# A linear attention with two MLPs: weight conversion two chunks at a time, its low parts on VectorE, and gate and attention first in the order

## The chip, the cores and the metric

The kernel runs on one core of one Trainium2 chip. Its time is device microseconds of one execution, median of three runs. The engines are PE (TensorE, with PEld for its weight loads), DVE (VectorE), ACT (ScalarE), POOL (GpSimd) and SP, whose queue issues the DMAs. Engines work through their own instruction lists in order and wait for each other by semaphores.

## The reference

```
q_s = exp(q - max(q, axis=-1));  q_s /= sum(q_s, -1) + 1e-9
k_s = exp(k - max(k, axis=2));   k_s /= sum(k_s, 2) + 1e-9
x   = q_s @ (k_s^T @ v)              # 4 batches, 8 heads, 576 rows, 64 wide
x   = x as (2304, 512)
h   = x @ moe_w_in;   x = (h - tanh(h)) @ moe_w_out       # 512 -> 2048 -> 512
h   = x @ moe2_w_in;  out = softplus(h) @ moe2_w_out
```

All inputs are float64 and the result is float32. The four weight matrices reach the chip as the raw bits of float64 (two 32-bit words a number).

## The kernel before

Every matmul that matters is done as three: an operand is split into a high and a low part (hi, lo, of a rounded 32-bit type), and lo\*hi, hi\*lo and hi\*hi are added up in PSUM.

**Weights.** A matrix comes in 16 chunks of 128 of the 2048 hidden features. A chunk of float64 words is 128 x 1024 words of 32 bits, 512 KB, and lies in one of six buffers of the tag `raw`. `convert` (lines 111 to 126) turns it into 128 x 512 float32 numbers in place by five passes: ACT (L121) reads the top 16 bits, DVE (L122) joins sign and exponent, DVE (L123) clamps, ACT (L124) scales, DVE (L125) shifts the low word in. `parts` (lines 128 to 133) adds a copy on ACT, which is the hi part (L131), and a subtraction, which is the lo part (L132). The lo part runs on POOL, but for every fourth chunk of the first input matrix, where it runs on DVE. `w_task` does a chunk of both matrices of the first MLP, `w2_out_task` a chunk of the last matrix, `w2_in_task` a pair of chunks of the second MLP's input matrix, from which it makes seven sums (a Strassen form) that go back to DRAM.

**Blocks.** The 2304 rows are worked through in five blocks of 512, 256, 512, 512 and 512 columns for the first MLP. A block has 16 steps, one a hidden chunk f: `hidden` (12 matmuls into PSUM tile h), `gate` (ACT tanh L332, DVE g L333, ACT hi part gh L334, DVE lo part gl L335), `mid_out` (12 matmuls into four accumulators x). The hidden product runs two steps ahead of `mid_out`. The first block needs each chunk of the first MLP's weights as it comes to it, so the conversions of the first MLP run beside block 0. The second MLP's input weights are converted beside the blocks that follow, and its output weights beside the last block, in which a converted chunk of the first MLP's output matrix gives up its place.

**Attention.** `kv_task` makes k^T v of a batch and a pair of heads: max over k (DVE L229, then a transposition pm on PE L232, DVE mx L234, a transposition pb L237), subtraction (DVE L239), exp (ACT L240), product pk (PE L244), its reciprocal r (DVE L246, L247), and kv (ACT L250). `x_task` makes a block's x from q: maximum and subtraction (L279, L281), exp (L282), sum (L285 to L287), qn (L289), transposition pt (PE L298), product px (L305), hi and lo part (ACT L307, DVE L308). Those of the first block run ahead of it (the prologue); those of the next block run beside the present one.

**Order.** Tasks are generators that go on by one `yield` a step. A scheduler then lays out each engine's list from the program's order, dependencies and buffers: what comes earlier in the program has the higher priority, and what has its inputs later in its reckoning moves behind. `tc.high_priority()` puts what it encloses ahead.

Of the kernel before, what the change touches and what calls it, by code (L numbers as in the profile page):

```python
# [19 lines left out]
def linear_attention_two_mlps(  # L20
# [28 lines left out]
    nc = tc.nc  # L49
# [39 lines left out]
    def f32(ap):  # L89
        return ap.bitcast(F32)  # L90
# [9 lines left out]
    def raw_tile(name):  # L100
        return main.tile([P, NC, 2 * P], U32, tag="raw", name=name, bufs=6)
# [6 lines left out]
    def load_out(raw, w_out, f):  # L108
        nc.sync.dma_start(out=raw.rearrange("p c f -> p (c f)"), in_=w_out[f * P : (f + 1) * P, :])

    def convert(raw):

        words = raw.rearrange("p c (f two) -> p c f two", two=2)
        y, x = words[:, :, :, 0], words[:, :, :, 1]
        top = raw.bitcast(U16).rearrange("p c (f four) -> p c f four", four=4)[:, :, :, 1]  # L120
# [17 lines left out]
    def w_task(f):
        raws = [raw_tile(f"raw{w}0_{f}") for w in "io"]
        load_in(raws[0], w1_in, f)  # L140
        load_out(raws[1], w1_out, f)
# [60 lines left out]
    def kv_task(b, hp, pool, bufs):  # L202
# [31 lines left out]
        nc.vector.tensor_reduce(mx, pm[:, :KP], axis=AX, op=ALU.max)  # L234
# [10 lines left out]
        r = pool.tile([P, 1], F32, tag="r", name=f"r{nm}", bufs=bufs)  # L245
        nc.vector.tensor_scalar(r, pk[:, P : P + 1], 1e-9, None, op0=ALU.add)  # L246
        nc.vector.reciprocal(r, r)  # L247
        for h in range(2):
            d = slice(h * D, (h + 1) * D)
            nc.scalar.mul(kv[b % 2, hp][d, d], pk[d, d], r[d])  # L250

# [7 lines left out]
    def x_task(i, hp, pool, bufs):  # L259
# [6 lines left out]
        while r0 < n:  # L266
# [28 lines left out]
        yield
# [228 lines left out]
    for f in range(NF):  # L524
        if f >= PRE:
# [166 lines left out]
```

## Time and profile before

| what | us |
|---|---|
| median of three runs | 892.52 (892.36 to 894.33) |
| the profiled execution, its own time | 893.67 |
| its span, first to last instruction | 891.9 |
| PE busy | 841.6 (94%) |
| DVE busy | 637.8 (72%) |
| ACT busy | 489.3 (55%) |
| POOL busy | 93.0 (10%) |

Shares over the whole span hide the stages. Beside block 0 (34 to 158 us) DVE is busy nearly all the time and PE is not; from 300 us to the end of the fourth block PE is busy all the time and DVE under half. A mean duration of a group mixes passes that ran alone with passes that ran beside POOL, so the rows below take one stretch with POOL at work and one without.

### The profile page before, as it was taken

What the parts mean: (1) busy time and instruction counts of PE and PEld (TensorE: products, weight loads), DVE (VectorE), ACT (ScalarE), POOL (GpSimd) and SP (SyncE); (2) the same over time, 40 slices, a digit from 0 to 9 for tenths busy, and PEclk for the clock granted to TensorE, in tenths of its full rate; (3) what the DMA queues carried; (4) which work ended last, traced back from release to release, by engine and by line L of the source; (5) the groups of instructions that cost most, each with busy time, mean ns of one, the idle gap of its engine ahead of it and who ended that gap; (6) DMA issues with size and microseconds to landing.
All of it is one profiled execution on the core that took longest, in us unless ns stands there. A gap on an engine that the chain in (4) does not pass through costs nothing.

```text
span 891.9 us, 11576 instructions
## 1 busy us (share of the span) xinstructions
PE 841.6 (94%) x4152; PEld 721.9 (81%) x4152; DVE 637.8 (72%) x990; ACT 489.3 (55%) x806; POOL 93.0 (10%) x88
## 2 busy tenths in 40 slices
PE   4788889999999999999998999999999999999997
PEld 3566768998888888888886888988899989898986
DVE  8899999899897444434697475667957669675664
ACT  4877776555665332223563565647556466655643
POOL 4243431000000000001242300000100000000000
PEclk9899999999999999999999999999999999999999
DMA  9565655876664210003427254343653444543421
GB/s 248 160 183 170 182 144 145 261 207 186 245 227 134 51 47 12 12 1 118 155 71 249 83 175 112 114 129 113 198 174 111 125 113 124 183 124 111 115 59 71
DMA packets 98616, 121.34 MB, mean 136 GB/s; under 512 B 38656, under 2 KB 62976, under 8 KB 98560
## 3 DMA queue, kind: packets, MB, share of 16 engines
q1 hardware_dynamic: 98560, 120.61, 44.9%
q8 instruction: 33, 0.54, 0.3%
q14 instruction: 23, 0.19, 0.1%
HBM read 96.47 MB, written 24.12 MB: 135 GB/s over the span
## 4 chain that ended last, share of the span: by engine, by line
PE 63%; DVE 15%; issue 8%; DMA 5%; ACT 5%; POOL 3%; SPq 0%; POOLq 0%; ACTq 0%; DVEq 0%
PE h L323 11%; PE one L418 10%; PE o L495 7%; PE o L496 7%; PE o L494 7%; PE seven L418 5%; PE x L352 4%; PE x L350 4%; PE x L351 4%; PE two L418 2%; POOL ol L132 2%; DVE m L229 2%; DVE g L333 1%; DMA rawi<-in_moe_w_in_dram 1%; DVE rawi L122 1%
## 5 line engine op out<-in xcount | busy, mean ns | idle before, releaser
L323 PE MATMUL h<-xh,il 128*128 128x512 f32 (+1 forms) x320 | 126.9, 397 | 9.7 <-DVE g L333 4.4
L323 PE MATMUL h<-xl,ih 128*128 128x512 f32 (+1 forms) x320 | 120.7, 377 | 0.8 <-DVE xl L308 0.8
L323 PE MATMUL h<-xh,ih 128*128 128x512 f32 (+1 forms) x320 | 120.6, 377 | 0.0
L350 PE MATMUL x<-gh,ol 128*128 128x512 f32 (+1 forms) x320 | 119.2, 372 | 0.9 <-DVE x2s L359 0.9
L352 PE MATMUL x<-gh,oh 128*128 128x512 f32 (+1 forms) x320 | 118.7, 371 | 0.0
L351 PE MATMUL x<-gl,oh 128*128 128x512 f32 (+1 forms) x320 | 118.7, 371 | 0.0
L418 PE MATMUL one<-xf,wf 128*128 128x384 f32 x576 | 116.8, 337 | 0.9 <-ACT u L433 0.9
L494 PE MATMUL o<-oh,gl 128*128 128x512 f32 x288 | 112.8, 392 | 2.3 <-DVE gl L479 1.8
L495 PE MATMUL o<-ol,gh 128*128 128x512 f32 x288 | 113.7, 395 | 0.0
L496 PE MATMUL o<-oh,gh 128*128 128x512 f32 x288 | 113.7, 395 | 0.0
L418 PEld LDWEIGHTS one<-xf,wf 128*128 128x128 f32 x576 | 103.0, 188 | 7.4 <-ACT u L433 1.4
L333 DVE TENSOR_TENSOR g<-h,g 128x512 f32<-128x512 f32 (+1 forms) x80 | 50.6, 632 | 53.1 <-ACT g L332 52.9
L332 ACT ACTIVATE g<-h 128x512 f32<-128x512 f32 (+1 forms) x80 | 44.0, 549 | 76.9 <-PE h L323 76.7
L470 DVE TENSOR_SCALAR u<-e 128x768 f32<-128x768 f32 x48 | 26.7, 557 | 80.0 <-ACT e L468 80.0
L323 PEld LDWEIGHTS h<-xh,il 128*128 128x128 f32 x320 | 62.0, 194 | 23.7 <-DVE g L333 5.9
L323 PEld LDWEIGHTS h<-xl,ih 128*128 128x128 f32 x320 | 62.0, 194 | 11.8 <-DVE xl L308 1.6
L478 ACT CAST gh<-e 128x768 fp32r<-128x768 f32 x48 | 40.2, 837 | 56.8 <-DVE e L475 56.2
L323 PEld LDWEIGHTS h<-xh,ih 128*128 128x128 f32 x320 | 61.6, 192 | 10.9
L350 PEld LDWEIGHTS x<-gh,ol 128*128 128x128 f32 x320 | 61.0, 191 | 11.5 <-DVE x2s L359 1.5
L352 PEld LDWEIGHTS x<-gh,oh 128*128 128x128 f32 x320 | 60.9, 190 | 10.2
L351 PEld LDWEIGHTS x<-gl,oh 128*128 128x128 f32 x320 | 60.8, 190 | 10.0
L335 DVE TENSOR_TENSOR gl<-g,gh 128x512 fp32r<-128x512 f32 (+1 forms) x80 | 53.3, 666 | 20.1 <-ACT gh L334 18.9
(97 smaller groups left out, 1534.5 us busy)
## 6 DMA issues: line engine op xcount, KB each, us to landing
wf<-forms SPq DMA_DIRECT2D x168, 256.0 KB, 2.7
rawi<-in_moe_w_in_dram SPq DMA_DIRECT2D x32, 512.0 KB, 4.3
rawo<-in_moe_w_out_dram SPq DMA_DIRECT2D x32, 512.0 KB, 3.4
forms<-stage SPq DMA_DIRECT2D x24, 512.0 KB, 3.2
v<-in_v_dram SPq DMA_DIRECT2D x32, 144.0 KB, 3.9
out_dram<-ot SPq DMA_DIRECT2D x18, 256.0 KB, 3.0
x2d<-x2s SPq DMA_DIRECT2D x16, 256.0 KB, 2.2
k<-in_k_dram SPq DMA_DIRECT2D x24, 144.0 KB, 3.5
```

Of the source, the lines that this page charges most:

```text
L323: nc.tensor.matmul(p, w[:, c], x[:, c, :n], start=at == 0, stop=at == 3 * NC - 1)
L332: tanh[0] = nc.scalar.activation(g, h, AF.Tanh)
L333: nc.vector.tensor_tensor(g, h, g, op=ALU.subtract)
L335: nc.vector.tensor_tensor(gl, g, f32(gh), op=ALU.subtract)
L350: nc.tensor.matmul(a, ol[:, s], gh, start=first, stop=False)
L351: nc.tensor.matmul(a, oh[:, s], gl, start=False, stop=False)
L352: nc.tensor.matmul(a, oh[:, s], gh, start=False, stop=last)
L418: nc.tensor.matmul(a, w[:, wp, c], x[:, xp, c], start=first and at == 0, stop=at == 5, skip_group_check=True)
L478: nc.scalar.copy(gh, e)
L494: nc.tensor.matmul(a, gl[:, c], oh, start=first, stop=False)
L495: nc.tensor.matmul(a, gh[:, c], ol, start=False, stop=False)
L496: nc.tensor.matmul(a, gh[:, c], oh, start=False, stop=last)
```

## The change

Pairs of chunks: `w_task(p)` now does chunks 2p and 2p+1. Where it can, it loads both chunks' words side by side into a tile that later holds another pair's converted weights (`IN_AT`, `OUT_AT`), and each pass of `convert` and `parts` then covers 1024 numbers in a partition and not 512. This holds for five pairs of the input matrix (p = 2 to 6) and six of the output matrix (p = 1 to 6); the other ten chunks keep passes of 512. It starts two steps earlier and converts in two halves. All lo parts of weights are on DVE. A pair of the last matrix shares one tile.

Order: the DVE and ACT work of `gate`, and that of `kv_task` and `x_task` outside the prologue, is enclosed in `tc.high_priority()`.

Maximum over k: one reduction over 768 elements in a partition becomes three elementwise maxima, of 384, 128 and 128. Line numbers shift: L122, L123, L125 become L124, L125, L127; L132 becomes L133; L333 and L335 become L388 and L390.

```diff
-    def parts(pool, w, m, f, x, eng):
-        nc.scalar.copy(hi, x)
-        eng.tensor_tensor(lo, x, f32(hi), op=ALU.subtract)
+    def parts(out, x):
+        nc.scalar.copy(out[0], x)
+        nc.vector.tensor_tensor(out[1], x, f32(out[0]), op=ALU.subtract)
...
+    IN_AT, OUT_AT = {2: 6, 3: 7, 4: 5, 5: 6, 6: 7}, {0: 4, 1: 5, 2: 6, 3: 7, 4: 5, 5: 6, 6: 7}
+    def w_task(p):
+        f = 2 * p
+        raws = []
+        for w, at_, pool_of in (("i", IN_AT, in_pool), ("o", OUT_AT, lambda _: weights_out)):
+            if p in at_:
+                tag = at_[p]
+                raw = pool_of(tag).tile([P, 2, 2 * DM], U32, tag=f"{w}{tag}", name=f"raw{w}0_{f}")
+                raws.append([raw[:, k] for k in range(2)] if p == 0 else [raw.rearrange("p k f -> p (k f)")])
...
+        yield
+        yield
+        if p:
+            yield
+            yield
...
+        for k in range(2):
+            for n, (t, raw) in enumerate(zip(made, raws)):
+                if len(raw) == 2:
+                    parts([part[:, k] for part in (t[:, 0], t[:, 1])], f32(convert(raw[k])[1]))
+                elif k == n:
+                    parts([part.rearrange("p k f -> p (k f)") for part in (t[:, 0], t[:, 1])], f32(convert(raw[0])[1]))
+            yield
...
     def w2_out_task(f):
-        wo[1, f] = tuple(map(whole, parts(weights_out, "o", 1, f, x, nc.gpsimd)))
+        if f % 2 == 0:
+            out2[f] = out2[f + 1] = weights_out.tile([P, 2, 2, DM], F32R, tag=f"o{f // 2}", name=f"o1_{f}")
+        wo[1, f] = tuple(out2[f][:, n, f % 2] for n in range(2))
+        parts(wo[1, f], f32(x))
...
+    def soon(pool):
+        return tc.high_priority() if pool is att else nullcontext()
...
-        nc.vector.tensor_reduce(m1, kt.rearrange("p j h d -> p h d j"), axis=AX, op=ALU.max)
+        with soon(pool):
+            nc.vector.tensor_tensor(m3, kt[:, : KJ // 2], kt[:, KJ // 2 :], op=ALU.max)
+            nc.vector.tensor_tensor(m1, m3[:, 0], m3[:, 1], op=ALU.max)
+            nc.vector.tensor_tensor(m1, m1, m3[:, 2], op=ALU.max)
...
-        tanh[0] = nc.scalar.activation(g, h, AF.Tanh)
-        nc.vector.tensor_tensor(g, h, g, op=ALU.subtract)
+        with tc.high_priority():
+            tanh[0] = nc.scalar.activation(g, h, AF.Tanh)
+            nc.vector.tensor_tensor(g, h, g, op=ALU.subtract)
...
-            at(0, f - 6, lambda f=f: w_task(f))
+            at(0, f - 8, lambda f=f: w_task(f // 2))
```

DVE, at the first k maximum that block 0 makes for the next block (m_0; the names carry chunk or head pair and a serial number). Before:

```order
L123 TENSOR_SCALAR rawo_5_445<-rawo_5_445 128x512
L229 TENSOR_REDUCE m_0_553<-k_0_492 96x128
L125 SCALAR_TENSOR_TENSOR rawi_5_444<-rawi_5_444 128x512
L125 SCALAR_TENSOR_TENSOR rawo_5_445<-rawo_5_445 128x512
L333 TENSOR_TENSOR g_3_575<-h_3_562,g_3_575 128x512
```

The same place now:

```order
L125 TENSOR_SCALAR rawi_6_399<-rawi_6_399 128x1024
L273 TENSOR_TENSOR m_0_527<-k_0_476 96x384
L124 SCALAR_TENSOR_TENSOR rawo_6_402<-rawo_6_402 128x1024
L274 TENSOR_TENSOR m_0_526<-m_0_527 96x128
L133 TENSOR_TENSOR o_4_462<-rawo_4_387,o_4_462 128x1024
L388 TENSOR_TENSOR g_4_602<-h_4_589,g_4_602 128x512
L329 TENSOR_REDUCE qm_0_579<-q_0_531 128x4
L275 TENSOR_TENSOR m_0_526<-m_0_526,m_0_527 96x128
```

The maximum stood after the passes of chunk 5 and ahead of gate 3; it now stands ahead of gate 4 and ends behind it, with the lo part o_4 between.

DVE, just ahead of the last gate of block 0 (g_15; rawi_4, rawi_5, rawi_6 with numbers above 2000, sums and stage belong to the second MLP's input weights). Before:

```order
L175 TENSOR_TENSOR sums_2389<-sums_2389,rawi_4_2210 128x256
L176 TENSOR_TENSOR sums_2389<-rawi_4_2210,rawi_5_2211 128x256
L177 TENSOR_TENSOR sums_2389<-rawi_4_2210,sums_2389 128x256
L279 TENSOR_REDUCE qm_0_1548<-q_0_1509 128x8
L246 TENSOR_SCALAR r_3_1339<-pk_3_1332 128x1
L188 TENSOR_TENSOR stage_0_2458<-rawi_4_2210,stage_0_2458 128x2x256
L247 RECIPROCAL r_3_1339<-r_3_1339 128x1
L281 TENSOR_TENSOR q_0_1509<-q_0_1509,qm_0_1548 128x512
L188 TENSOR_TENSOR stage_1_2507<-sums_2389,stage_1_2507 128x2x256
L285 TENSOR_REDUCE qsum_0_1588<-q_0_1509 128x8
L122 SCALAR_TENSOR_TENSOR rawi_6_2419<-rawi_6_2419 128x512
L333 TENSOR_TENSOR g_15_1362<-h_15_1349,g_15_1362 128x512
```

The same place now:

```order
L133 TENSOR_TENSOR o_14_1032<-rawo_15_825,o_14_1032 128x512
L275 TENSOR_TENSOR m_0_1390<-m_0_1390,m_0_1391 96x128
L125 TENSOR_SCALAR rawi_4_2105<-rawi_4_2105 128x512
L124 SCALAR_TENSOR_TENSOR rawi_5_2106<-rawi_5_2106 128x512
L125 TENSOR_SCALAR rawi_5_2106<-rawi_5_2106 128x512
L127 SCALAR_TENSOR_TENSOR rawi_4_2105<-rawi_4_2105 128x512
L388 TENSOR_TENSOR g_15_1245<-h_15_1232,g_15_1245 128x512
```

Ahead of this gate the second MLP had seven passes over chunks 4 to 6, four sums and two stage passes; now it has five passes over chunks 4 and 5, and the rest comes later.

ACT, in the last block at the tanh of chunk 14 (rawo_0 and rawo_15 are words of the last matrix; oh and o its hi parts). Before:

```order
L334 CAST gh_13_4187<-g_13_4186 128x512
L121 ACTIVATE rawo_0_4366<-rawo_0_4366 128x512
L131 CAST oh_11_4252<-rawo_11_4124 128x512
L124 ACTIVATE rawo_0_4366<-rawo_0_4366 128x512
L332 ACTIVATE g_14_4229<-h_74_4216 128x512
```

The same place now:

```order
L132 CAST o_10_4103<-rawo_10_3982 128x512
L132 CAST o_10_4103<-rawo_11_4024 128x512
L126 ACTIVATE rawo_15_4198<-rawo_15_4198 128x512
L387 ACTIVATE g_14_4126<-h_74_4113 128x512
L389 CAST gh_14_4127<-g_14_4126 128x512
L123 ACTIVATE rawo_0_4258<-rawo_0_4258 128x512
L123 ACTIVATE rawo_2_4295<-rawo_2_4295 128x512
L126 ACTIVATE rawo_0_4258<-rawo_0_4258 128x512
L387 ACTIVATE g_15_4171<-h_75_4158 128x512
```

The tanh of chunk 14 stood behind both passes over rawo_0; it now stands ahead of them, and the tanh of chunk 15 behind rawo_0 and rawo_2. The two hi parts of a pair come together.

## Rows read from the trace of the kernel before

**Rows 1.** Busy us by stretch: PE, PEld, DVE, ACT, POOL; clock, DMA share, GB/s.

```profile
0.00:34.00 34.00, 16.28 (x80) 11.96 (x80) 27.48 (x53) 21.24 (x39) 13.13 (x29) 0.97 0.89 224
34.00:158.00 124.00, 107.47 (x481) 86.61 (x482) 120.43 (x201) 85.57 (x156) 41.68 (x31) 0.94 0.57 166
158.00:225.00 67.00, 63.34 (x481) 59.55 (x481) 61.07 (x133) 40.31 (x86) 0.43 (x4) 1.00 0.70 214
...
300.00:450.00 150.00, 150.00 (x671) 122.69 (x670) 67.07 (x107) 53.58 (x91) 8.12 (x6) 1.00 0.17 57
450.00:490.00 40.00, 35.61 (x149) 28.43 (x148) 33.05 (x37) 20.81 (x34) 15.08 (x8) 0.96 0.46 160
```

**Rows 2.** Timeline of PE: start, duration, instruction, idle before and releaser.

```profile
34.17 1.22 PE L323 MATMUL h<-xh,il 128*128 128x512 f32 x2 [4.20 <-POOL il L132]
...
58.71 0.30 PE L232 MATMUL pm<-ident,m 96*128 96x96 f32 x1 [3.20 <-DVE m L229]
...
79.24 0.41 PE L298 MATMUL pt<-ident,qn 128*128 128x128 f32 x2 [3.94 <-DVE r L247]
```

**Rows 3.** DVE groups by line, 34 to 158 us: busy, mean ns, idle before.

```profile
L122 DVE SCALAR_TENSOR_TENSOR rawi<-rawi 128x512 uint32<-128x512 uint32 x18 | 16.5, 917 | 0.0
L125 DVE SCALAR_TENSOR_TENSOR rawi<-rawi 128x512 uint32<-128x512 uint32 x18 | 15.8, 880 | 0.4 <-ACT rawi L124 0.3
L335 DVE TENSOR_TENSOR gl<-g,gh 128x512 fp32r<-128x512 f32 (+1 forms) x17 | 13.6, 801 | 0.9 <-ACT gh L334 0.8
L123 DVE TENSOR_SCALAR rawi<-rawi 128x512 f32<-128x512 f32 x18 | 13.1, 726 | 0.0
L125 DVE SCALAR_TENSOR_TENSOR rawo<-rawo 128x512 uint32<-128x512 uint32 x15 | 11.9, 796 | 0.0
L333 DVE TENSOR_TENSOR g<-h,g 128x512 f32<-128x512 f32 (+1 forms) x18 | 11.7, 651 | 1.6 <-ACT g L332 1.6
L122 DVE SCALAR_TENSOR_TENSOR rawo<-rawo 128x512 uint32<-128x512 uint32 x14 | 10.6, 759 | 0.0
...
L123 DVE TENSOR_SCALAR rawo<-rawo 128x512 f32<-128x512 f32 x14 | 6.4, 454 | 0.0
```

**Rows 4.** DVE groups by line, 140 to 230 us, where POOL is idle.

```profile
L122 DVE SCALAR_TENSOR_TENSOR rawi<-rawi 128x512 uint32<-128x512 uint32 x11 | 7.5, 686 | 0.2 <-ACT rawi L121 0.2
...
L123 DVE TENSOR_SCALAR rawi<-rawi 128x512 f32<-128x512 f32 x11 | 4.6, 422 | 0.1
```

**Rows 5.** Timeline of POOL near 41 us.

```profile
40.77 1.32 POOL L132 TENSOR_TENSOR il<-rawi,ih 128x512 fp32r<-128x512 f32 x1 [3.39 <-ACT ih L131]
```

**Rows 6.** Timeline of DVE near 41 us.

```profile
40.80 1.57 DVE L123 TENSOR_SCALAR rawi<-rawi 128x512 f32<-128x512 f32 x1
```

**Rows 7.** Timeline of DVE near 47 us and near 465 us.

```profile
47.29 0.68 DVE L122 SCALAR_TENSOR_TENSOR rawi<-rawi 128x512 uint32<-128x512 uint32 x1
47.89 0.68 DVE L122 SCALAR_TENSOR_TENSOR rawo<-rawo 128x512 uint32<-128x512 uint32 x1
...
464.45 0.94 DVE L384 TENSOR_TENSOR xf<-xs,xf 128x768 fp32r<-128x768 f32 x1
465.32 0.41 DVE L123 TENSOR_SCALAR rawo<-rawo 128x512 f32<-128x512 f32 x1
```

**Rows 8.** Timeline of the prologue: DVE and the queue of SP.

```profile
4.25 5.51 DVE L229 TENSOR_REDUCE m<-k 96x128 f32<-96x768 f32 x4 [4.25 <-DMA k<-in_k_dram]
...
11.99 3.38 SPq L209 DMA_DIRECT2D v<-in_v_dram  x4
```

**Rows 9.** Timeline of ACT near 471 us.

```profile
471.08 0.68 ACT L121 ACTIVATE rawo<-rawo 128x512 uint32<-128x512 uint16 x1 [3.22 <-DMA rawo<-in_moe_w_out_dram]
...
474.57 0.58 ACT L332 ACTIVATE g<-h 128x512 f32<-128x512 f32 x1
```

**Rows 10.** Timeline of POOL near 464 us.

```profile
463.90 3.88 POOL L132 TENSOR_TENSOR ol<-rawo,oh 128x512 fp32r<-128x512 f32 x1 [4.67 <-ACT oh L131]
```

**Rows 11.** Timeline of PE near 476 us.

```profile
476.04 0.80 PE L323 MATMUL h<-xh,il 128*128 128x512 f32 x1 [2.91 <-DVE g L333]
```

More of the change, by code (lines that the diff above doesn't have):

```diff
@@ L1 @@
 import itertools
-from contextlib import ExitStack
+from contextlib import ExitStack, nullcontext
 import concourse.bass as bass
@@ L108, in load_out @@
     def load_out(raw, w_out, f):
-        nc.sync.dma_start(out=raw.rearrange("p c f -> p (c f)"), in_=w_out[f * P : (f + 1) * P, :])
+        nc.sync.dma_start(out=raw, in_=w_out[f * P : (f + 1) * P, :])
     def convert(raw):
-        words = raw.rearrange("p c (f two) -> p c f two", two=2)
-        y, x = words[:, :, :, 0], words[:, :, :, 1]
-        top = raw.bitcast(U16).rearrange("p c (f four) -> p c f four", four=4)[:, :, :, 1]
+        words = raw.rearrange("p (f two) -> p f two", two=2)
+        y, x = words[:, :, 0], words[:, :, 1]
+        top = raw.bitcast(U16).rearrange("p (f four) -> p f four", four=4)[:, :, 1]
         nc.scalar.activation(y, top, AF.Copy, scale=2.0**-13, bias=2.0**-14 - 0.5)
@@ L138, in w_task, with in_pool @@
[L138 to L141, printed above, removed]
+        return y, x
+    def parts(out, x):
+        nc.scalar.copy(out[0], x)
+        nc.vector.tensor_tensor(out[1], x, f32(out[0]), op=ALU.subtract)
+    def in_pool(p):
+        return weights["first" if p < 2 else "last" if p >= 6 else "mid"]
+    IN_AT, OUT_AT = {2: 6, 3: 7, 4: 5, 5: 6, 6: 7}, {0: 4, 1: 5, 2: 6, 3: 7, 4: 5, 5: 6, 6: 7}
[7 more added lines that the diff above has]
+                raws.append([raw[:, k] for k in range(2)] if p == 0 else [raw.rearrange("p k f -> p (k f)")])
+                each = [raw[:, k] for k in range(2)]
+            else:
+                each = [raw_tile(f"raw{w}0_{f + k}").rearrange("p c f -> p (c f)") for k in range(2)]
+                raws.append(each)
+            for k in range(2):
+                if w == "i":
+                    load_in(each[k].rearrange("p (c f) -> p c f", c=NC), w1_in, f + k)
+                else:
+                    load_out(each[k], w1_out, f + k)
@@ L142, in w_task @@
         yield
         yield
-        pool = weights["first" if f < 4 else "last" if f >= 12 else "mid"]
-        wi[f] = parts(pool, "i", 0, f, convert(raws[0]), nc.vector if f % 4 == 0 else nc.gpsimd)
-        wo[0, f] = tuple(map(whole, parts(weights_out, "o", 0, f, convert(raws[1]), nc.gpsimd)))
+        if p:
+            yield
+            yield
+        made = []
+        for w, pool in (("i", in_pool(p)), ("o", weights_out)):
+            made.append(pool.tile([P, 2, 2, DM], F32R, tag=f"{w}{p}", name=f"{w}0_{f}"))
@@ new lines, in w_task @@
+        for k in range(2):
+            wi[f + k] = tuple(made[0][:, n, k].rearrange("p (c f) -> p c f", c=NC) for n in range(2))
+            wo[0, f + k] = tuple(made[1][:, n, k] for n in range(2))
+        for k in range(2):
+            for n, (t, raw) in enumerate(zip(made, raws)):
[4 more added lines that the diff above has]
+            yield
@@ L148, in w2_out_task @@
     def w2_out_task(f):
-        raw = raw_tile(f"rawo1_{f}")
+        raw = raw_tile(f"rawo1_{f}").rearrange("p c f -> p (c f)")
         load_out(raw, w2_out, f)
@@ L166, in w2_in_task @@
         yield
-        w0 = convert(raws[0])
+        w0, w1 = (raw.rearrange("p c (f two) -> p c f two", two=2)[:, :, :, 1] for raw in raws)
+        w0, w1 = f32(w0), f32(w1)
+        convert(raws[0].rearrange("p c f -> p (c f)"))
         yield
-        w1 = convert(raws[1])
+        convert(raws[1].rearrange("p c f -> p (c f)"))
         yield
@@ L233, in kv_task @@
         mx = pool.tile([P, 1], F32, tag="mx", name=f"mx{nm}", bufs=bufs)
-        nc.vector.tensor_reduce(mx, pm[:, :KP], axis=AX, op=ALU.max)
+        with soon(pool):
+            nc.vector.tensor_reduce(mx, pm[:, :KP], axis=AX, op=ALU.max)
         yield
@@ L238, in kv_task @@
         most = pb[:KP, :P].rearrange("p (h d) -> p h d", h=2).unsqueeze(1).to_broadcast([KP, KJ, 2, D])
-        nc.vector.tensor_tensor(ke, kt, most, op=ALU.subtract)
-        nc.scalar.activation(ke, ke, AF.Exp)
+        with soon(pool):
+            nc.vector.tensor_tensor(ke, kt, most, op=ALU.subtract)
+            nc.scalar.activation(ke, ke, AF.Exp)
         yield
@@ L245, in kv_task @@
         r = pool.tile([P, 1], F32, tag="r", name=f"r{nm}", bufs=bufs)
[L246 to L250, printed above, removed]
+        with soon(pool):
+            nc.vector.tensor_scalar(r, pk[:, P : P + 1], 1e-9, None, op0=ALU.add)
+            nc.vector.reciprocal(r, r)
+            for h in range(2):
+                d = slice(h * D, (h + 1) * D)
+                nc.scalar.mul(kv[b % 2, hp][d, d], pk[d, d], r[d])
     xt = {}
@@ L299, in x_task @@
         qs = pool.tile([P, n], F32, tag="qs", name=f"qs{nm}", bufs=bufs)
-        nc.scalar.copy(qs, pt[:, :n])
+        with soon(pool):
+            nc.scalar.copy(qs, pt[:, :n])
         yield
@@ L551, in linear_attention_two_mlps @@
     tasks |= {f"x{hp}": x_task(0, hp, pro, NHP) for hp in range(NHP)}
-    tasks |= {f"w{f}": w_task(f) for f in range(PRE)}
-    order = """k0 k1 k2 k3 x0 x1 x2 x3 k0 k0 k1 k1 w0 k2 k3 k2 k3 x1 k0 x0 k1 k0 x0 w0 x2 k2 x2 x3 x1 x3 w1 k3 w1 k1 x0 k2 x1 k3 x2 x3 x0 w0 x2 x3 w1 x1"""
+    tasks["w"] = w_task(0)
+    order = """k0 k1 k2 k3 x0 x1 x2 x3 k0 k0 k1 k1 w k2 k3 k2 k3 x1 k0 x0 k1 k0 x0 w x2 k2 x2 x3 x1 x3 k3 k1 x0 k2 x1 k3 x2 x3 x0 w x2 x3 w x1"""
     for n, name in enumerate(order.split()):
```

50 lines of the change are left out of this document (25 added, 25 removed).

## The prediction

> **What bounds the kernel now.** I read the shares of the span first, then busy time by stretch, then PE's idle times with their releasers, then DVE's groups in a stretch with POOL at work and in one without. By stretch [rows 1] PE works all 150 us from 300 to 450, so there only PE's work counts and DVE's 67.07 us are hidden. From 34 to 158 us it is DVE that works 120.43 of 124 us, while PE works 107.47: 16.5 us idle, and 0.06 x 124 = 7.4 us more lost to the granted clock of 0.94. From 158 to 225 PE lacks 3.7 us, from 450 to 490 it lacks 4.4 us and 0.04 x 40 = 1.6 us of clock. Elsewhere there is nothing that this change can reach but the prologue. So the most that can be won is 23.9 + 3.7 + 6.0 = 33.6 us, nearly all of it beside block 0.
>
> What PE waits for there is small attention work that stands in DVE's list behind conversions: 3.20 us for a k maximum, 3.94 us for a reciprocal [rows 2]. And DVE is not slow by its own work alone. The same pass L122 of 128 x 512 takes 917 ns on average beside block 0 and 686 where POOL is idle, the clamp L123 726 against 422 [rows 3, 4]. A single case shows how: POOL's lo part runs from 40.77 for 1.32 us, DVE's clamp begins at 40.80, takes 1.57 us and so ends just behind it [rows 5, 6].
>
> **The change part by part, beside block 0.**
>
> *POOL's lo parts go, and with them the stretching.* Against the clean 686 ns (two tensors read) and 422 ns (clamp) the groups of rows 3 are too long by: L122 rawi 18 x 231 = 4.2, L125 rawi 18 x 194 = 3.5, clamp rawi 18 x 304 = 5.5, gl 17 x 115 = 2.0, L125 rawo 15 x 110 = 1.7, L122 rawo 14 x 73 = 1.0, clamp rawo 14 x 32 = 0.4; in all 18.3 us. Bounds: 0 if the stretching has another cause, 18.3 if all is POOL's; I take 18.3, since the clean rows are the same passes on the same tiles.
>
> *DVE gets 28 lo parts.* Passes of 512 follow each other at 0.60 us (47.29, 47.89), one of 768 takes 0.87 us of the engine (464.45 to 465.32) [rows 7]. That is 0.27 for 256 elements and 0.06 fixed. A pass of 1024 isn't in the trace: between 0.87 and 2 x 0.60 = 1.20; by the slope 1.14, which I take. Eleven merged lo parts cost 12.5, ten single ones 6.0, and four of the latter's number were on DVE already (2.4): +16.1 us (13.2 to 16.8).
>
> *Merged conversions.* Eleven pairs by three DVE passes save 0.06 each: -2.0 us. (The merge itself is worth only 33 + 11 = 44 fixed parts, 2.6 us.) [...]
>
> *Maximum over k.* L229 takes 5.51 / 4 = 1.38 us [rows 8]; passes of 384 and twice 128 are by the slope 0.46 + 2 x 0.20 = 0.86 (not below 0.18, their fixed parts, and not above 3 x 0.60). Four of them: -2.1 us.
>
> *Work that leaves the stretch.* Ahead of gate 15 stood seven passes over the second MLP's words (five of 0.60, two clamps of 0.33, which need half the time for an element), four sums of 256 (0.33) and two stage passes (0.60), 6.2 us; now three of 0.60 and two of 0.33, 2.5 us. They come later, beside blocks 2 and 3, where 300 to 450 us has 83 us of DVE free [rows 1] to hide them: -3.7 us. Without that cover they would come back one for one.
>
> The sum is -18.3 + 16.1 - 2.0 - 2.1 - 3.7 = -10.0 us on an engine that bounds the stretch; PE's own floor there is 124 - 23.9 = 100 us, so it permits that. Bounds for this term: -3 (ACT holds it up, below) to -20 (PE near its floor).
>
> *Gate and attention first.* With DVE still the bound, priority does not shorten DVE's list; it decides what PE finds late. Its worth I put where DVE is not quite the bound, at 158 to 225 us: of PE's 3.7 idle us, on k maxima and the like, 2 go (0 to 3.7). What is late next there is the second MLP's conversion, which nobody waits for yet.
>
> *Prologue.* Four maxima win 2.1 us of DVE, but the loads of v for head pairs 2 and 3 (queue, 11.99 us) now stand behind two chunks more, 1 MB, which at 224 GB/s is 4.7 us [rows 1, 8]. They gate the last two kv and x products. The queue on SP moves the same loads otherwise, later ones earlier. POOL's il that PE awaited at 34.17 [rows 2] is replaced by a DVE pass. I take 0 (-2 to +4).
>
> **The last block.** At 463.90 POOL's lo part takes 3.88 us under DVE's load [rows 10] and frees its raw buffer that much later; the next words come late, ACT waits 3.22 us for them at 471.08, the tanh behind runs at 474.57 [rows 9], and PE idles 2.91 us to 476.04 [rows 11]. Without POOL's pass the buffer is freed sooner, and in the new order that tanh stands ahead of the words. Against it: a pair's tile needs both steps of block 4 done, so the first chunk's buffer is held a step longer, and the next tanh stands behind two such loads. The sixteen lo parts cost DVE 9.6 us over some 90 us, of which rows 1 show 7 of 40 free. Of 6.0 us I take 3 (0 to 6).
>
> **Sum.** The profiled execution took 893.67, 1.2 above the median of 892.52. 893.67 - 10.0 - 2 - 3 = 878.7, as a median 877.5. Forecast 877, its own range 867 to 884.
>
> **The rivals.**
>
> *A, ACT holds it up.* Merged passes keep ACT too. L121 takes 0.68 [rows 9]; one of two chunks may keep a tanh or hi part waiting 0.68 longer. ACT is busy 85.57 of 124 us [rows 1], so of 32 such instructions of block 0 each finds on average half a pass ahead with a chance of 0.69: 32 x 0.34 x 0.69 = 7.5 us given back, 885. For it: DVE, ACT and PE would all be near full. Against: tanh and hi part stand first in the order.
>
> *B, PE's floor.* If attention and gates come so early that PE finds all ready, all 33.6 us go: 859. For it: the waits of rows 2 are on attention passes. Against: by the sum above DVE still has 110 us of work for this stretch.
>
> *C, slower: DVE is overloaded.* If DVE's passes are long for another reason than POOL, the lo parts come on top: +16.1 - 2.0 - 2.1 - 3.7 = +8.3 beside block 0, and the last block keeps its waits: 901. It decides if a 512 pass of L124 or L127 still takes over 0.8 us with POOL idle. Against it: gate g (L333), one of whose operands lies in PSUM, has 651 ns beside the same POOL work while gl has 801 [rows 3]. [...]
>
> *D, no change.* The buffers that hold later weights are filled first, a pair comes a step late, and PE waits for conversions as much as it now waits for attention. Then the 12 us beside blocks 0 and 1 do not come, 889.5, and without the last block's 3 it is 892.5. For it: a pair of 1024 is ready later than its first chunk alone was. Against: conversion starts two steps earlier.
>
> **How the numbers follow.** Forecast 0.58, A 0.20, B 0.10, C 0.06, D 0.06. The range leaves out most of B and C: 862 to 889. A measurement of this kernel tells 0.3% (2.7 us) from no change, so faster is below 889.8. Faster: 0.58 + 0.10 + A but for its tail, 0.87; same: D and A's tail, 0.07; slower: 0.06.
>
> **What would show it.** POOL idle from 25 to 400 us but for memsets; L124 and L127 of 512 near 690 ns and of 1024 near 1.2 us; DVE still over 90% busy beside block 0, which ends some 10 us sooner; PE's idle time there down to about half; PE without an idle time of 2 us near 470. The forecast is wrong if the 512 passes stay above 0.8 us, if PE waits more than 10 us in all for passes L133 on i tiles, or if ACT's waits grow by as much as DVE's shrink.

## The result and the profile after

The changed kernel takes 867.66 us (median of four, 866.98 to 868.74) against 892.52; the ratio is 0.9718, with a 95% interval of 0.9701 to 0.9736. Its profiled execution took 868.74, with a span of 867.0. The forecast was 877, with a range of 862 to 889. The direction and the places were right, and all three terms of the sum were too small.

The end of a block is read here as the start of DVE's first pass that takes its sum out of PSUM (x2s). Differences to before:

| end of | before | after | difference | forecast, cumulative |
|---|---|---|---|---|
| block 0 | 157.85 | 143.29 | -14.6 | -10 |
| block 1 | 224.60 | 206.50 | -18.1 | -12 |
| block 2 | 324.59 | 306.63 | -18.0 | -12 |
| block 3 | 417.14 | 399.21 | -17.9 | -12 |
| block 4 | 509.17 | 484.38 | -24.8 | -15 |
| span | 891.9 | 867.0 | -24.9 | -15 |

So the time was won beside blocks 0 and 1 and in the last block, and nowhere else. Busy time by stretch after, the columns as in [rows 1], to which these rows answer:

```profile
0.00:34.00 34.00, 18.83 (x83) 13.39 (x84) 26.98 (x64) 20.64 (x37) 10.64 (x27) 0.90 0.84 224
34.00:158.00 124.00, 116.66 (x584) 96.39 (x582) 114.84 (x205) 87.47 (x136) 0.56 (x4) 0.97 0.55 168
158.00:225.00 67.00, 66.92 (x456) 61.05 (x455) 57.36 (x136) 39.26 (x81) 0.42 (x4) 1.00 0.65 206
300.00:450.00 150.00, 150.00 (x663) 122.76 (x662) 75.27 (x117) 60.65 (x101) 5.01 (x2) 1.00 0.19 67
450.00:490.00 40.00, 40.00 (x188) 34.38 (x187) 26.07 (x39) 20.87 (x36) 2.17 (x1) 1.00 0.53 180
```

POOL falls from 41.68 to 0.56 us beside block 0. PE lacks 0.1 us where it lacked 3.7, and nothing where it lacked 4.4. DVE's 75.27 us for 67.07 at 300 to 450 are no added work: blocks end 18 us sooner, so this window holds more of the last block's conversion. By blocks, the work that left blocks 0 and 1 shows in block 2, which is as long as before. Before, and after:

```profile
224.60:324.59 99.99, 99.30 (x472) 81.64 (x471) 72.65 (x139) 50.53 (x91) 0.32 (x3) 1.00 0.44 142
206.50:306.63 100.13, 99.15 (x474) 81.78 (x473) 79.48 (x166) 56.75 (x102) 0.32 (x3) 1.00 0.57 189
```

DVE's groups after, from 34 us to the end of block 0, the columns as in [rows 3]:

```profile
L388 DVE TENSOR_TENSOR g<-h,g 128x512 f32<-128x512 f32 x16 | 10.9, 684 | 3.5 <-ACT g L387 3.3
L390 DVE TENSOR_TENSOR gl<-g,gh 128x512 fp32r<-128x512 f32 x16 | 10.9, 683 | 0.9 <-ACT gh L389 0.9
L133 DVE TENSOR_TENSOR o<-rawo,o 128x1024 fp32r<-128x1024 f32 x6 | 7.3, 1218 | 0.8 <-ACT o L132 0.8
...
L124 DVE SCALAR_TENSOR_TENSOR rawi<-rawi 128x1024 uint32<-128x1024 uint32 x5 | 6.1, 1216 | 0.0
...
L127 DVE SCALAR_TENSOR_TENSOR rawi<-rawi 128x512 uint32<-128x512 uint32 x6 | 4.1, 681 | 0.0
L124 DVE SCALAR_TENSOR_TENSOR rawi<-rawi 128x512 uint32<-128x512 uint32 x5 | 3.4, 683 | 0.0
...
L125 DVE TENSOR_SCALAR rawi<-rawi 128x512 f32<-128x512 f32 x5 | 2.1, 422 | 0.0
...
L341 DVE TENSOR_TENSOR qn<-q,qsum 128x256 f32<-128x256 f32 x4 | 1.7, 418 | 0.0
```

Every pass has its clean duration: 683 ns where [rows 3] have 917, 880 and 801, and 422 for the clamp's 726. DVE now waits for ACT's tanh (3.3 us), which [rows 3] showed for 1.6.

PE's idle times of 0.5 us and more after, from 20 to 145 us, the columns as in [rows 2]:

```profile
28.01 5.49 PE L358 MATMUL px<-qs,kv 128*128 128x512 f32 x6 [3.14 <-ACT kv L299]
39.55 0.50 PE L377 MATMUL h<-xh,i 128*128 128x512 f32 x1 [0.57 <-DVE i L133]
46.87 0.50 PE L377 MATMUL h<-xh,i 128*128 128x512 f32 x1 [1.01 <-DVE i L133]
93.19 0.27 PE L278 MATMUL pm<-ident,m 96*128 96x96 f32 x1 [1.74 <-DVE m L275]
96.60 2.51 PE L292 MATMUL pk<-v,k 96*128 96x130 f32 x10 [2.42 <-ACT k L288]
```

The wait of 4.20 us for POOL's il is gone; in its place, 6 us earlier, PE waits 3.14 us for kv. Of the waits of [rows 2], the longest for a maximum is 1.74 us for 3.20, and those for a reciprocal are gone; the wait for k (its exp on ACT, 2.42 us) is new. From 410 to 490 us PE has no idle time, so the chain of [rows 9 to 11] has no successor; at the end of that stretch DVE waits for PE:

```profile
484.38 0.69 DVE L414 TENSOR_SCALAR x2s<-x 128x512 f32<-128x512 f32 x1 [3.55 <-PE x L407]
```

### The profile page after: what moved, and what is told of

The parts are those of the page before. It is cut to its first block, busy times and chain, and to the rows that moved or that the text cites. A ratio compares the mean times of both kernels' runs of the same rounds, so it can differ in the third digit from the quotient of the medians.

```text
span 867.0 us, 11425 instructions
## 1 busy us (share of the span) xinstructions
PE 836.3 (96%) x4152; PEld 718.9 (83%) x4152; DVE 620.7 (72%) x1022; ACT 486.2 (56%) x773; POOL 25.2 (3%) x44
## 4 chain that ended last, share of the span: by engine, by line
PE 82%; DVE 7%; ACT 5%; DMA 4%; issue 1%; SPq 0%; ACTq 0%; DVEq 0%
PE h L377 20%; PE one L473 10%; PE o L550 7%; PE o L551 7%; PE o L549 7%; PE x L407 7%; PE x L405 6%; PE x L406 6%; PE seven L473 5%; PE two L473 3%; PE px L358 2%; PE pk L292 2%; DMA xs<-x2d 1%; DMA k<-in_k_dram 1%; DMA x2d<-x2s 1%
## 5 line engine op out<-in xcount | busy, mean ns | idle before, releaser
L377 PE MATMUL h<-xh,i 128*128 128x512 f32 (+1 forms) x640 | 200.1, 379 | 1.6 <-DVE i L133 1.6
L377 PEld LDWEIGHTS h<-xh,i 128*128 128x128 f32 x640 | 117.4, 189 | 24.5 <-DVE i L133 3.2
L405 PE MATMUL x<-gh,o 128*128 128x512 f32 (+1 forms) x320 | 118.2, 372 | 0.8 <-ACT x2s L412 0.8
L407 PE MATMUL x<-gh,o 128*128 128x512 f32 (+1 forms) x320 | 118.8, 371 | 0.0
L406 PE MATMUL x<-gl,o 128*128 128x512 f32 (+1 forms) x320 | 118.6, 371 | 0.0
L377 PE MATMUL h<-xl,i 128*128 128x512 f32 (+1 forms) x320 | 118.2, 369 | 0.0
L549 PE MATMUL o<-o,gl 128*128 128x512 f32 x288 | 112.6, 391 | 2.6 <-DVE gl L534 2.2
L550 PE MATMUL o<-o,gh 128*128 128x512 f32 x288 | 113.7, 395 | 0.0
L551 PE MATMUL o<-o,gh 128*128 128x512 f32 x288 | 113.6, 395 | 0.0
L388 DVE TENSOR_TENSOR g<-h,g 128x512 f32<-128x512 f32 (+1 forms) x80 | 50.6, 632 | 59.2 <-ACT g L387 58.8
L377 PEld LDWEIGHTS h<-xl,i 128*128 128x128 f32 x320 | 60.5, 189 | 11.1 <-issue 1.5
L405 PEld LDWEIGHTS x<-gh,o 128*128 128x128 f32 x320 | 60.5, 190 | 10.8 <-ACT x2s L412 1.0
L406 PEld LDWEIGHTS x<-gl,o 128*128 128x128 f32 x320 | 60.6, 189 | 10.2 <-DVE gl L390 0.4
L407 PEld LDWEIGHTS x<-gh,o 128*128 128x128 f32 x320 | 60.6, 189 | 10.1
L390 DVE TENSOR_TENSOR gl<-g,gh 128x512 fp32r<-128x512 f32 (+1 forms) x80 | 50.9, 637 | 19.4 <-ACT gh L389 18.8
```

The costliest lines, as they stand in the source:

```text
L377: nc.tensor.matmul(p, w[:, c], x[:, c, :n], start=at == 0, stop=at == 3 * NC - 1)
L405: nc.tensor.matmul(a, ol[:, s], gh, start=first, stop=False)
L406: nc.tensor.matmul(a, oh[:, s], gl, start=False, stop=False)
L407: nc.tensor.matmul(a, oh[:, s], gh, start=False, stop=last)
L549: nc.tensor.matmul(a, gl[:, c], oh, start=first, stop=False)
L550: nc.tensor.matmul(a, gh[:, c], ol, start=False, stop=False)
```

## Experiments

The theory: POOL's lo parts stretch DVE's passes, and that DVE is rid of this is nearly all of the gain. The rivals: that gate and attention go first; that pairs and merged passes do it; that POOL's lo part itself came late and others waited for it.

### One part alone, or all but one

**lo_dve**, the kernel before with all weight lo parts on DVE:

```diff
-        eng.tensor_tensor(lo, x, f32(hi), op=ALU.subtract)
+        nc.vector.tensor_tensor(lo, x, f32(hi), op=ALU.subtract)
```

> The kernel before, with the lo parts of all weight chunks on DVE and nothing else changed. Theory S (POOL's lo parts stretch DVE's passes): the 512-wide passes L122 and L125 beside block 0 fall from 917 and 880 ns to 690; 22 us of stretching go and 28 lo parts at 0.60 us come (16.8), so block 0 ends about 5 us sooner, and with the wait of PE near 474 us gone the time is 886 to 890. Rival P (the gain comes from gate and attention going first): DVE only gets more work in the old order, so 895 to 905. Rival M (the gain comes from pairs and merged passes): the place of the lo parts is worth nothing, 892 to 894.

Measured: 874.28 us, ratio 0.9761 (0.9740 to 0.9782). This one line brings five sixths of the change's gain, more than the theory's own estimate. DVE's groups in lo_dve, 34 to 150 us:

```profile
L125 DVE SCALAR_TENSOR_TENSOR rawi<-rawi 128x512 uint32<-128x512 uint32 x16 | 11.0, 687 | 0.5 <-ACT rawi L124 0.3
L122 DVE SCALAR_TENSOR_TENSOR rawi<-rawi 128x512 uint32<-128x512 uint32 x16 | 10.9, 683 | 0.0
...
L132 DVE TENSOR_TENSOR il<-rawi,ih 128x512 fp32r<-128x512 f32 x14 | 9.6, 685 | 1.1 <-ACT ih L131 1.0
...
L123 DVE TENSOR_SCALAR rawi<-rawi 128x512 f32<-128x512 f32 x16 | 6.7, 419 | 0.0
```

All clean, with the program otherwise as before. Block 0 ends at 147.49 (-10.4), block 1 takes 3.2 us less, and block 4 takes 85.1 us where it took 92.0: in the last block, lo_dve has the whole of the change's gain.

**prio**, the kernel before with gate and attention first (the k maximum left as one reduction), lo parts on POOL; and **after_pool**, the changed kernel with its lo parts on POOL:

```diff
+        with tc.high_priority():
             tanh[0] = nc.scalar.activation(g, h, AF.Tanh)
...
+        with soon(pool):
             nc.vector.tensor_reduce(mx, pm[:, :KP], axis=AX, op=ALU.max)
```

```diff
-        nc.vector.tensor_tensor(out[1], x, f32(out[0]), op=ALU.subtract)
+        nc.gpsimd.tensor_tensor(out[1], x, f32(out[0]), op=ALU.subtract)
```

> The kernel before, with gate and attention work (outside the prologue) put first in the order and nothing else changed; lo parts stay on POOL. Theory S: DVE still has about 120 us of stretched work beside block 0, so block 0 ends within 4 us of before and the time is 888 to 892. Rival P: the order alone removes most of PE's waits for k maxima, reciprocals and qn, so 16.5 us of idle PE beside block 0 fall below 9 and the time is 872 to 882. Rival M: 891 to 893.

> The changed kernel with all weight lo parts back on POOL. Theory S: the 512-wide passes of L124 and L127 beside block 0 rise from 690 ns to above 850 and the 1024-wide ones from 1.22 to above 1.5 us; DVE loses 28 lo parts (16 us) but gets about 20 us of stretching, and POOL's own passes of about 2.6 us for 1024 come late for PE: 875 to 890. Rival P: 866 to 869. Rival M: 866 to 869, or below where DVE is relieved of its lo parts.

Measured: prio 893.22, ratio 0.9972 (0.9955 to 0.9990), block 0 ends at 157.95. after_pool 894.48, ratio 0.9991 (0.9975 to 1.0007). The order alone gives 2.5 us, no more than the theory said; after_pool is slower than any of its forecasts. So all of the rest of the change, with lo parts on POOL, is worth nothing that can be measured. DVE's groups in after_pool, 34 to 150 us:

```profile
L127 DVE SCALAR_TENSOR_TENSOR rawo<-rawo 128x1024 uint32<-128x1024 uint32 x6 | 9.4, 1570 | 0.0
L124 DVE SCALAR_TENSOR_TENSOR rawi<-rawi 128x1024 uint32<-128x1024 uint32 x5 | 7.5, 1492 | 0.0
...
L125 DVE TENSOR_SCALAR rawo<-rawo 128x1024 f32<-128x1024 f32 x6 | 6.3, 1048 | 0.0
...
L341 DVE TENSOR_TENSOR qn<-q,qsum 128x256 f32<-128x256 f32 x4 | 4.9, 1237 | 0.0
```

1217 ns have become 1492 and 1570, the clamp's 682 are 1048, and qn's 418 are 1237. The rivals that the order or the merging carries the gain are refuted by these two.

**after_noprio**, the changed kernel with no priority on gates and attention:

```diff
     def soon(pool):
-        return tc.high_priority() if pool is att else nullcontext()
+        return nullcontext()
...
-        with tc.high_priority():
+        with nullcontext():
             tanh[0] = nc.scalar.activation(g, h, AF.Tanh)
```

> The changed kernel without gate and attention first in the order. Theory S, with DVE no longer full in every microsecond: PE's waits for k maxima, reciprocals and gates come back in part, block 0 ends 3 to 6 us later, block 1 about 3 us more: 871 to 877. Rival P: the whole gain beside block 0 goes, 882 to 890. Rival M: 867 to 869.

Measured: 866.26, ratio 0.9665 (0.9627 to 0.9703). Only rival M, for which the priorities were worth nothing, came near: without them the changed kernel is no slower, and by its ratio a little faster. It is taken up again below.

### Is it POOL's traffic, or POOL's lateness?

lo_dve takes away two things at once: POOL's accesses to SBUF, and the wait for a lo part that POOL makes slowly (beside block 0 POOL's ol and il take 1581 and 1568 ns on average in the kernel before, DVE's 687 and 685 in lo_dve). **lo_two** and **lo_one** give back the first alone. They are lo_dve with POOL passes over each hi part of the first MLP's chunks, whose result nobody reads. Each of the two kernels has one of the last two lines:

```diff
+        if m == 0:
+            for at_ in range(0, DM, 256):
+                scratch = att.tile([P, 256], F32, tag="scratch", name="scratch", bufs=1)
+                part = f32(hi).rearrange("p c f -> p (c f)")[:, at_ : at_ + 256]
+                nc.gpsimd.tensor_tensor(scratch, part, part, op=ALU.subtract)     # lo_two
+                nc.gpsimd.tensor_scalar(scratch, part, 2.0, None, op0=ALU.mult)   # lo_one
```

> lo_dve (the kernel before with all weight lo parts on DVE) plus idle work on POOL: for each chunk of the first MLP, as soon as its hi part is there, POOL subtracts the hi part from itself in two passes of 128x256 (two SBUF operands) into a scratch tile that nobody reads or waits for. Theory S (POOL's traffic stretches DVE's passes, whatever POOL computes): the 512-wide passes L122 and L125 beside block 0 rise from 685 ns to above 820, block 0 ends 10 to 20 us later than in lo_dve, and the time is 884 to 896. Rival W (lo_dve won because nothing waits any more for POOL's slow lo part): POOL is in nobody's way, passes stay at 685 ns, 872 to 877.

> As lo_two, but POOL multiplies the hi part by 2 (one SBUF operand) in the same two passes of 128x256. Theory S in its general form (any POOL access to SBUF collides): passes rise as in lo_two, 884 to 896. Theory S in its narrow form (POOL's pass of one operand leaves room): passes stay within 685 to 750 ns, 873 to 879. Rival W: 872 to 877.

Measured: lo_two 888.88, ratio 0.9920 (0.9893 to 0.9948); lo_one 877.87, ratio 0.9796 (0.9755 to 0.9836). The stretch from 34 us to the end of block 0, columns as in [rows 1]: first lo_dve,

```profile
34.00:147.49 113.49, 106.06 (x480) 85.23 (x480) 107.24 (x209) 80.04 (x147) 0.42 (x4) 0.95 0.55 162
```

then lo_one,

```profile
34.00:150.26 116.26, 105.58 (x480) 83.75 (x479) 113.24 (x209) 80.33 (x147) 84.20 (x63) 0.96 0.54 158
```

then lo_two:

```profile
34.00:161.28 127.28, 110.52 (x479) 86.79 (x478) 125.63 (x209) 80.87 (x147) 65.10 (x63) 0.92 0.49 145
```

DVE does 209 instructions in each. They take 107.24 us beside an idle POOL, 113.24 beside 84 us of POOL passes of one operand, and 125.63 beside 65 us of POOL passes of two. The block's end moves by +2.8 and +13.8, less than that, since DVE's idle time in the stretch falls from 6.3 us to 3.0 and 1.7. Nobody reads what POOL makes here (one hi part on ACT waits 1.3 us for a POOL pass, in lo_one and lo_two alike), so beside block 0 the rival of the late lo part falls: traffic is enough. Which passes are hit is in DVE's groups of lo_two, 34 to 150 us:

```profile
L132 DVE TENSOR_TENSOR ol<-rawo,oh 128x512 fp32r<-128x512 f32 x15 | 14.0, 936 | 0.0
...
L122 DVE SCALAR_TENSOR_TENSOR rawi<-rawi 128x512 uint32<-128x512 uint32 x14 | 11.3, 810 | 0.0
...
L338 DVE TENSOR_TENSOR g<-h,g 128x512 f32<-128x512 f32 x14 | 9.5, 677 | 0.0
L123 DVE TENSOR_SCALAR rawi<-rawi 128x512 f32<-128x512 f32 x14 | 8.6, 614 | 0.0
...
L290 DVE TENSOR_REDUCE qsum<-q 128x4 f32<-128x256 f32 x4 | 1.6, 404 | 0.0
```

Against lo_dve, passes that read two SBUF tensors are long (L122 810 ns for 683, ol 936 for 687), and so is the clamp (614 for 419), which reads one and with POOL idle takes 422 where L122 takes 686 [rows 4]. g, with one operand in PSUM (677 for 683), and the reductions (qsum 404 for 410) are not. In size, POOL's passes of one SBUF operand cost DVE 6.0 us for 84 us of POOL's time, those of two 18.4 for 65. It is no fixed price: in the kernel before, 41.7 us of POOL cost some 21.8 (worked out below).

### What the merged passes are worth

**after_split**, the changed kernel with the same tiles and loads, each pass over half a pair:

```diff
-                    parts([part.rearrange("p k f -> p (k f)") for part in (t[:, 0], t[:, 1])], f32(convert(raw[0])[1]))
+                    for half in range(2):
+                        s = slice(half * 2 * DM, (half + 1) * 2 * DM)
+                        parts([part[:, half] for part in (t[:, 0], t[:, 1])], f32(convert(raw[0][:, s])[1]))
```

> The changed kernel with the same tiles, loads and times of the pairs, but every pass of conversion and parts over 512 numbers, not 1024. By the spacing of passes (0.06 us fixed a pass) the 44 more passes on DVE cost 2.6 us, so 868 to 872 where the changed kernel has 867.7. [...] Rival A (merged passes hold up gates on ACT and DVE): splitting is no loss or a gain, 863 to 868.

Measured: 877.46, ratio 0.9792 (0.9758 to 0.9827), 0.0084 over the repeat of the changed kernel below, or 7.5 us. That is nearly three times the 2.6. By their durations above (2 x 683 - 1216 ns) passes would have a fixed part of 0.15 us each, 6.6 us for 44, which would come near, but the spacing of passes doesn't bear it out. DVE in the changed kernel, near 66 us:

```profile
65.60 1.22 DVE L127 SCALAR_TENSOR_TENSOR rawi<-rawi 128x1024 uint32<-128x1024 uint32 x1
66.74 0.17 DVE L338 RECIPROCAL qsum<-qsum 128x4 f32<-128x4 f32 x1
```

A pass of 1024 takes 1.14 us of the engine, as the slope said, against 2 x 0.60 for two of 512. So 2.6 of the 7.5 us are fixed parts of DVE's passes. The split kernel's DVE also does more of the next blocks' attention ahead of block 0's end (6 k subtractions for 4, 3 xl of 512 for 1), since its order came out otherwise. By the spacings this is an estimated 7 us, and with the 2.6 it makes up the 9.4 us that DVE is busy longer up to the block's end (112.01 for 102.58), which comes 8.5 us later. Block 1 is then 2.4 us shorter, and block 2 is 2.8 longer. Why the work done early is not won back there is not settled.

### The order

**lo_prio**, the kernel before with both lo parts on DVE and the priorities of prio:

> The kernel before with both all weight lo parts on DVE and gate and attention work first in the order. After the first runs I expect that the order adds nothing to the move of the lo parts: 872 to 877, as lo_dve (874.3). Rival P2 (the order pays once POOL no longer stretches DVE, and the rest of the changed kernel's gain is this): 866 to 870. Rival N (the order costs, as the faster run without it suggests): 876 to 880.

Measured: 881.82, ratio 0.9840 (0.9796 to 0.9883), against lo_dve's 0.9761: rival N, and more of it, as the order costs some 7 us. DVE's idle times of 1.1 us and more in lo_prio, 34 to 158 us:

```profile
39.45 0.69 DVE L346 TENSOR_TENSOR g<-h,g 128x512 f32<-128x512 f32 x1 [1.17 <-ACT g L345]
71.31 1.52 DVE L233 TENSOR_REDUCE m<-k 96x128 f32<-96x768 f32 x1 [1.10 <-DMA k<-in_k_dram]
100.53 1.49 DVE L233 TENSOR_REDUCE m<-k 96x128 f32<-96x768 f32 x1 [2.29 <-DMA k<-in_k_dram]
109.41 0.42 DVE L294 TENSOR_REDUCE qsum<-q 128x4 f32<-128x256 f32 x1 [1.23 <-ACT q L290]
```

Put first, a maximum stands at the head of DVE's list before its k has landed, and the conversions behind it wait too; lo_dve has no wait for k here. Up to the end of block 0, which comes 7.7 us later than in lo_dve, DVE is idle 4.7 us longer (3.4 of it for k) and does 3.0 us more work, attention of the next blocks. The last four runs shared a chip: **after_again** is the changed kernel, **noprio_again** repeats after_noprio, and **gate_only** drops the priority of attention alone:

```diff
     def soon(pool):
-        return tc.high_priority() if pool is att else nullcontext()
+        return nullcontext()
```

> The changed kernel as it is, on the same chip as the three that follow, so that they can be compared: ratio to the kernel before 0.970 to 0.974, 867 to 872.

> The changed kernel without gate and attention first in the order, once more, beside the changed kernel on one chip. Theory N (being first costs a little: a prioritised instruction whose input is not there yet holds up its engine's whole list): 2 to 5 us less than the changed kernel, ratio 0.964 to 0.969. Rival O (no difference, the chips differ): within 1.5 us of it.

> The changed kernel with only the gates first in the order and attention work in its old place. If attention's priority is what costs (its inputs come by DMA and by PE in small steps), the time is as without any priority, 862 to 867; if the gates' is, as the changed kernel, 867 to 871.

Measured: after_again 868.35, ratio 0.9708 (0.9677 to 0.9739); noprio_again 864.67, 0.9676 (0.9639 to 0.9712); gate_only 864.86, 0.9665 (0.9632 to 0.9697). Attention's priority thus costs the changed kernel 3.5 us by the medians (868.05 to 869.31 against 862.76 to 866.14); the intervals of the ratios overlap at their edges, so that it doesn't help is sure, and that it costs is likely. The gates' priority does nothing that can be measured. Without attention's, block 0 ends at 137.36 (gate_only) and not 143.36, of which 2.2 us are lost again beside block 2. Both versions are faster than the kernel before, and likely faster than the changed one. Up to the end of block 0, first after_again, then gate_only:

```profile
34.00:143.36 109.36, 103.66 (x479) 84.06 (x479) 102.56 (x177) 78.47 (x117) 0.51 (x4) 0.97 0.54 162
34.00:137.36 103.36, 99.45 (x475) 80.50 (x474) 96.50 (x161) 76.35 (x112) 0.43 (x4) 1.00 0.57 166
```

So here the priority does not cost what it cost in lo_prio. DVE is idle no longer (6.8 and 6.9 us); it does 16 passes more, 6.1 us, nearly all of them attention of later blocks, and block 1 is no shorter for it (63.4 and 63.5 us). PE has a lower granted clock at the same time (0.97 for 1.00) and 1.8 us more of idle time; what each of these gives to the 6 us is not separated.

Taken together: the lo parts alone give 0.9761, all the rest without them (after_pool, priorities included) 0.9991, and both without priorities (after_noprio) 0.9665. Once POOL's lo parts are gone, pairs, merged passes and split maxima thus bring another 8.0 us (874.28 to 866.26); beside POOL's lo parts the rest brought nothing.

**noprio_v** is noprio_again with v of head pairs 2 and 3 loaded ahead of the first words, to take the 3.14 us at 28 us too. Its edit against noprio_again:

```diff
-    order = """k0 k1 k2 k3 x0 x1 x2 x3 k0 k0 k1 k1 w k2 k3 k2 k3 x1 ...
+    order = """k0 k1 k2 k3 x0 x1 x2 x3 k0 k0 k1 k1 k2 k3 w k2 k3 x1 ...
```

> The changed kernel without priorities, and in the prologue the loads of v for head pairs 2 and 3 ahead of the loads of the first two chunks' words. In the changed kernel PE waits 3.1 us near 28 us for kv of these head pairs, whose reciprocals stand on DVE behind six passes of conversion. Theory V: the reciprocals come first, the products px start some 4 us sooner, the first chunk's i tile is ready at about the same time, and block 0 starts 1 to 3 us sooner: 860 to 865. Rival: the words come 3 us later and the i tile then is what PE waits for, no gain: 864 to 868.

Measured: 867.57, ratio 0.9700 (0.9667 to 0.9732), no gain. PE in noprio_v:

```profile
34.71 0.80 PE L377 MATMUL h<-xh,i 128*128 128x512 f32 x1 [6.67 <-DVE i L133]
```

The wait for kv has gone, and one for the i tile has come that is twice as long: the rival was right.

## Why the prediction was right, and where it was off

- **What bounds.** DVE beside block 0, and DVE's passes long because of POOL: shown by lo_dve, after_pool and lo_two.
- **POOL's stretching, -18.3.** The mechanism held. The sum left out q and qn, which [rows 3] don't list: they had 746 and 960 ns for 4 passes each and now have 414 and 418, another 3.5 us.
- **28 lo parts, +16.1; merged conversions, -2.0; k maxima, -2.1.** The unit durations came as worked out (a spacing of 1.14 for 1024). Two of the 28 ran ahead of 34 us, which leaves 14.9, and five maxima lie in the stretch, not four: -2.6. The maximum's passes have 549, 280 and 278 ns; no run undid them alone.
- **Work that leaves the stretch, -3.7.** This was the term most mis-sized. Up to the end of block 0, not only to gate 15, the kernel before does three chunks' joins and clamps, two chunks' shifts, six sums and four stage passes more than the changed one: 5 x 0.60 + 3 x 0.33 + 6 x 0.33 + 3 x 0.60 + 0.33 = 8.1 us. In lo_dve, which has neither pairs nor priorities, 5.9 us of the same work leave, so most of it does not need the new order.
- **The sum beside block 0.** The changed kernel does four passes of 512 more of later x tasks there, one gate pass of 256 less, and one shift of an output chunk less, which ran ahead of 34 us: +1.5. The sum by these counts is -18.3 - 3.5 + 14.9 - 2.0 - 2.6 - 8.1 + 1.5 = -18.1; DVE's busy time from 34 us to the block's end fell from 120.28 to 102.58, by 17.7. Its idle time there rose from 3.6 to 6.7, so the block ended 14.6 sooner. Before, and after:

```profile
34.00:157.85 123.85, 107.32 (x481) 86.46 (x482) 120.28 (x200) 85.55 (x155) 41.68 (x31) 0.94 0.57 166
34.00:143.29 109.29, 102.72 (x478) 83.12 (x477) 102.58 (x178) 78.36 (x117) 0.56 (x4) 0.97 0.54 162
```

  That 3.1 is not rival A's, although DVE waits for ACT's tanh: where it waits longest, ACT itself waits for PE's h.

```profile
105.18 0.69 DVE L388 TENSOR_TENSOR g<-h,g 128x512 f32<-128x512 f32 x1 [2.53 <-ACT g L387]
104.55 0.60 ACT L387 ACTIVATE g<-h 128x512 f32<-128x512 f32 x1 [3.92 <-PE h L377]
```

  PE had just been idle for the maximum (1.74 us) and for k (2.42 us). Then its granted clock was 0.50, and its matmuls of 512 columns followed each other at 0.43 us, up to 101.4 us; from 101.5 us the clock was 0.97, and they followed at 0.23.

```profile
98.80:101.40 2.60, 2.60 (x8) 2.09 (x8) 2.60 (x5) 1.22 (x1) 0.00 (x0) 0.50 0.00 0
101.50:104.20 2.70, 2.70 (x13) 2.25 (x12) 1.15 (x2) 0.00 (x0) 0.00 (x0) 0.97 0.19 49
```

- **Gate and attention first, -2 beside block 1.** The step that failed. Block 1 did take 3.5 us less, but lo_dve, without priorities, has 3.2 of these; by gate_only attention's priority more likely takes time than gives it. The prediction asked only what PE finds late in block 1. It left out that work put first moves into the stretch that DVE bounds (6.1 us in after_again), and that it may stand waiting for its own input (3.4 us in lo_prio).
- **Last block, -3 of 6.0.** It is 6.9: all of it went. lo_dve, where the block takes 85.1 us, shows that taking the lo parts off POOL is enough for it; whether by their lateness, as [rows 9 to 11] suggest, or by their traffic, no run separates. The changed kernel takes 85.2, so the later release of a pair's tile, held against it, cost nothing that shows.
- **Prologue, 0.** Block 0's first hidden product starts at 32.51 and not 34.17, -1.7; the loads of v that stand later cost the 3.14 us at 28 us, but in noprio_v, which has them first, the words come later and PE waits longer (6.67 us for i).
- **Rivals.** C (over 0.8 us a pass with POOL idle) fell on 683 ns. B's floor of 859 was not reached: of 16.5 idle us of PE beside block 0, 6.6 are left. D's waits for i tiles came to 1.6 us. The list of what would show it held, with DVE 94% busy, but for its sizes: the block ended 14.6 us sooner, not some 10, and PE's idle time fell to 40%, not half. PE's clock there rose only from 0.94 to 0.97.

## What to carry to other kernels

Before work is put on POOL to relieve DVE, compare DVE's mean duration of one pass in a stretch with POOL at work and in one without; here 28 passes that saved DVE 16 us cost it 22. Give priority to an instruction only if its inputs are there by then, since at the head of an engine's list it holds up all that stands behind it (3.4 us of DVE for k in lo_prio), and not to work that can wait when the stretch it moves into is bound by its own engine (6.1 us more of DVE's work in after_again). When work is said to leave a stretch, count it up to the event that ends the stretch.

## What was not expected of the hardware

POOL's own passes vary in length too. In lo_two its subtraction of 128x256 took 0.61 us at its shortest and 4.49 at its longest:

```profile
62.17 4.49 POOL L137 TENSOR_TENSOR scratch<-ih 128x256 f32<-128x256 f32 x1 [3.75 <-ACT ih L131]
```

A long POOL pass need not go with long DVE passes: in the kernel before, beside the 3.88 us of [rows 10], DVE's xf took 0.94 us and its clamp 0.41 [rows 7], where all 15 such xf took 942 to 959 ns and the clamp 422 with POOL idle [rows 4]. One operand was not quicker than two: a multiplication by a constant took POOL 0.85 us at its shortest in lo_one. On average, from 34 to 150 us, it took 1378 (oh) and 1460 ns (ih), where the subtraction took 953 and 1240.

And a stretched pass isn't lengthened by a constant share: in after_pool the mean of qn went from 418 to 1237 ns and that of L124 on 512 only from 683 to 701. The mean of qn is that of four passes of 2.62, 1.50, 0.41 and 0.41 us; the first two ran beside a POOL pass, the others beside none. The first:

```profile
80.40 2.62 DVE L341 TENSOR_TENSOR qn<-q,qsum 128x256 f32<-128x256 f32 x1
79.89 2.85 POOL L133 TENSOR_TENSOR i<-rawi,i 128x1024 fp32r<-128x1024 f32 x1 [2.37 <-ACT i L132]
```

So a DVE pass that meets a POOL pass may be lengthened by most of that pass: here 2.62 us for 0.41 beside 2.85 of POOL, and in the kernel before the clamp's 1.57 for 0.42 beside 1.32 [rows 4 to 6].
